# Joint x/gradient tile, an earlier reload of x, and stores issued by GpSimd and ScalarE, in a forward-and-backward block kernel

## The chip, the cores and the metric

The kernel runs on one core of a Trainium2 chip. The metric is device time in microseconds (us) from one launch to its end, median of several runs. A profiled execution gives a trace of every engine: TensorE (PE in the profile, its weight loads PEld), VectorE (DVE), ScalarE (ACT), GpSimd (POOL) and SyncE (SP). SP does no arithmetic here; it issues DMAs, one after the other in program order, and a DMA that must wait holds up all that stand behind it in SP's queue. The same holds for DMAs that ScalarE or GpSimd issue, in their own queues, with their arithmetic among them.

## The reference

The forward pass normalises x over its 512 features and adds three things: x itself, a gated long convolution over 2048 positions, and a gated bilinear feed-forward block. The kernel returns the output and the gradients of x, k, v, the two convolution kernels, the skip vector and the three weight matrices.

```python
def _A_ref(q, k, v, shift_k, ssm_k, ssm_D):
    k_shift = ...                      # 4-tap causal filter of k with shift_k
    kv = k_shift * v
    kv_f = rfft(pad(kv)); kf_f = rfft(pad(ssm_k))
    y = irfft(kv_f * kf_f)[:S]         # causal convolution over all 2048 positions
    y = y + kv * ssm_D
    return q * y

def _B_ref(x, w_gate, w_up, w_down):   # 512 -> 1376 -> 512
    h = (x @ w_gate) * (x @ w_up)
    return h @ w_down

xn = _layernorm(A_q)
out = A_q + _A_ref(xn, A_k, A_v, A_shift_k, A_ssm_k, A_ssm_D) + _B_ref(xn, B_w_gate, B_w_up, B_w_down)
# returned: out, and the vjp of out with grad_out for all inputs but B_x
```

All tensors are bf16; x, k, v and the gradient are 2048 x 512.

## The kernel before

The 2048 positions are laid out as 128 partitions with 16 rows each (`R`), and worked in 8 blocks of two rows (256 positions). Loads and stores of x, k, v, the gradient and the four results of that shape go through `load_rows` and `store_rows` (L212, L216): each is two DMAs of 64 partitions, issued by SP.

**Front.** For each block b, `load_q` and `load_go` (L299, L304) bring x and the gradient into tiles `x_b` and `go_b`; `norm_stats`, `norm_std` and `norm_rows` normalise x in place, and `store_xn` (L351) writes it to the DRAM scratch `XN`. `pre` (L380) multiplies gradient and normalised x (`dy_b`), filters k (`ks_b`, with the scratch tile `t_b`, stored to `KS`), and multiplies it by v (`v_b`). `stage1` (L364) runs the first stage of a two-stage Fourier transform by matmuls (`pf`), copies it to `fst` and stores it to the scratch `FD`. `kernel_spec` does the same for the convolution kernel, transposed by TensorE into tiles `kn`. `Tables` builds the sine tables on the chip: `W1` for the first stage, `EF` and `EI` for the second, `IW` for the inverse; `inverse_phases` does its part on GpSimd.

**Feed-forward.** For each block `ch`, `load_xt` (L486) brings normalised x and gradient transposed into `xt` and `gt` with transposing DMAs, from `x_b` and `go_b` while they are there, otherwise from `XN` and from the gradient's input tensor. The first two blocks are transposed by TensorE (`pe_t`, L469). `ffn1` multiplies by the three weights (`pgu`, `pdh`), forms the hidden values `hd` and stores them to the scratch `HDD`. `yb` (L543), which comes for block ch - 1 in the middle of `ffn1(ch)`, first reloads x into `xb` (one buffer), and then, for each of two halves, runs 11 matmuls of the down projection (`py`), adds x on VectorE (L554, into `bx`), and runs 22 matmuls of the gradient of the normalised x (`px`, L559). `bx` is stored to the scratch `BX`. `py` and `px` share two PSUM buffers.

**Second stage.** `groups` loads `X` from `FD`, transforms it (`ps`, `SP`), forms three products on VectorE (`T`, `U`, in `g_mul`), transforms back (`pg`, `GO`) and stores to the scratch `GD`. A generator interleaves this with the feed-forward work in TensorE's program order.

**Last phase.** When `ffn1` of the last block is done (tag `"wa"`), the gradient (`goC`) and `XN` (`xnC`) are loaded whole, 2 MB each (L884 to 887). Then `dw` (L1017) forms the three weight gradients, one block of 128 hidden features (`fb`) after another: `hb` holds all hidden values of that block, loaded from `HDD` (L787, two buffers), TensorE transposes them (`pt`, L843) and ScalarE copies them to `nath` and `natd`; `pd` and `pu` are the gradients, copied by ScalarE to `od` and `og` and stored by SP (L1007, L1046; `og` has one buffer and is stored after every second block). The last three blocks use transposing DMAs instead (`natT`, L797). Between these, `inv_y` and `inv_dk` load `GD` (`g1`, shown as `g`), transform it by matmuls (`pq`, `po`), and form `yC`, `dks` and the gradient of v (`kb`, in the buffer of the loaded `KS`, two buffers); `load_kh` loads k again (`khC`) for the gradient of the filter (`pk`); `final` (L1100) forms the output (`o`, one buffer) and the gradient of x (`e`, one buffer) with `bb`, loaded from `BX`; `bwd` (L1079) forms the gradient of k (`dk`, two buffers). `final` and `bwd` run wholly on VectorE, alternating, in `ew`; a rough order among generators is set by step counts (L1159), and a few DMAs are pinned behind another instruction (`issue_after`).

The program gives each DMA one of eight completion semaphores in turn. SP's and ScalarE's DMAs share one set of eight, and GpSimd's have their own. In the compiled order a DMA therefore also waits until the one eight before it in its set has landed.

## Time and profile before

| | us |
|---|---|
| median of 3 runs (lowest to highest) | 534.7 (534.37 to 536.45) |
| the profiled execution | 535.96 |
| its span, first to last instruction | 534.2 |
| TensorE busy | 480.1 (90%) |
| VectorE busy | 344.6 (65%) |
| ScalarE busy | 319.9 (60%) |
| GpSimd busy | 19.1 (4%) |

| moved by DMA | |
|---|---|
| all | 139.89 MB, mean 262 GB/s |
| queue of SP | 137.85 MB, 84.6% of the time of 16 DMA engines |
| queue of ScalarE | 1.36 MB, 1.0% |

The shares are averages over stages of quite different kinds. The front lasts till about 150 us, the interleaved second stage and feed-forward till about 345 us, and the last phase from there to the end. The profile cuts the span into 40 slices of 13.4 us and gives for each the busy share of every engine in tenths (9 is 90% or more), the clock granted to TensorE (PEclk), and the share of time in which the DMA engines were busy. A time line gives start, length, engine, line and operation, and in brackets the idle time of the engine ahead of it with what ended that idle time. SPq is SP's queue: its rows are the issues of DMAs, and a long one holds time in which the sequencer was held up.

### The profile page before, as it was taken

What the parts mean: (1) busy time and instruction counts of PE and PEld (TensorE: products, weight loads), DVE (VectorE), ACT (ScalarE), POOL (GpSimd) and SP (SyncE); (2) the same over time, 40 slices, a digit from 0 to 9 for tenths busy, and PEclk for the clock granted to TensorE, in tenths of its full rate; (3) what the DMA queues carried; (4) which work ended last, traced back from release to release, by engine and by line L of the source; (5) the groups of instructions that cost most, each with busy time, mean ns of one, the idle gap of its engine ahead of it and who ended that gap; (6) DMA issues with size and microseconds to landing.
All of it is one profiled execution on the core that took longest, in us unless ns stands there. A gap on an engine that the chain in (4) does not pass through costs nothing.

```text
span 534.2 us, 10803 instructions
## 1 busy us (share of the span) xinstructions
PE 480.1 (90%) x4438; PEld 316.4 (59%) x4438; DVE 344.6 (65%) x614; ACT 319.9 (60%) x354; POOL 19.1 (4%) x28
## 2 busy tenths in 40 slices
PE   6979999839993999999999999899987864999997
PEld 6957664414541664745736753366665644887776
DVE  5865777967828255777777776102246957797991
ACT  3757697734742677878969975176665512263332
POOL 9300000000000000000000000020000000000000
PEclk9989999987996999999999999899999997899999
DMA  9989966878799585997878469987999899969997
GB/s 249 337 250 260 312 213 213 294 216 294 255 337 254 191 239 192 269 259 250 231 254 291 151 173 306 371 302 219 356 330 331 272 214 312 333 147 261 259 243 235
DMA packets 106735, 139.89 MB, mean 262 GB/s; under 512 B 34715, under 2 KB 80192, under 8 KB 105150
## 3 DMA queue, kind: packets, MB, share of 16 engines
q1 hardware_dynamic: 105102, 137.85, 84.6%
q10 hardware_dynamic: 1584, 1.36, 1.0%
q8 instruction: 34, 0.56, 0.4%
q14 instruction: 15, 0.12, 0.1%
HBM read 68.45 MB, written 63.41 MB: 247 GB/s over the span
## 4 chain that ended last, share of the span: by engine, by line
PE 56%; DMA 15%; SPq 4%; ACT 2%; DVE 2%; issue 1%; DVEq 0%; ACTq 0%
PE pu L1035 12%; PE pgu L515 10%; PE px L559 10%; PE py L552 5%; PE pd L999 5%; DMA hb<-HDD 4%; PE pdh L521 4%; PE pt L843 3%; DMA g<-GD 3%; DMA khC<-in_A_k_dram 3%; DMA GD<-GO 2%; PE pg L617 2%; PE ps L588 2%; DMA xb<-in_A_q_dram 2%; SPq L497 2%; PE po L975 1%
## 5 line engine op out<-in xcount | busy, mean ns | idle before, releaser
L559 PE MATMUL px<-WT,hd 128*128 128x512 bf16 (+1 forms) x352 | 85.8, 394 | 15.3 <-DVE bx L554 14.7
L1035 PEld LDWEIGHTS <-xnC 128*128 128x128 bf16 x704 | 67.0, 98 | 9.0 <-issue 2.0
L559 PEld LDWEIGHTS <-hd 128*128 128x128 bf16 (+1 forms) x352 | 33.6, 101 | 61.3 <-issue 28.5
L1035 PE MATMUL pu<-natd,xnC 128*128 128x256 bf16 x512 | 58.3, 273 | 0.0
L234 ACT CAST GO<-pg 128x1024 bf16<-128x1024 f32 x48 | 46.2, 1015 | 15.4 <-issue 6.7
L604 DVE TENSOR_TENSOR T<-SP 128x2048 bf16<-128x2048 bf16 x24 | 29.4, 1223 | 38.8 <-ACT SP L234 38.8
L515 PE MATMUL pgu<-xt,Wu 128*128 128x256 bf16 (+1 forms) x352 | 53.9, 276 | 0.2 <-ACT gu L234 0.2
L234 ACT CAST gu<-pgu 128x1024 bf16<-128x1024 f32 (+1 forms) x48 | 45.3, 945 | 13.4 <-PE pgu L515 12.2
L515 PE MATMUL pgu<-xt,Wg 128*128 128x256 bf16 (+1 forms) x352 | 53.3, 274 | 0.0
L234 ACT CAST SP<-ps 128x1024 bf16<-128x1024 f32 x48 | 46.4, 1027 | 9.8 <-PE ps L588 7.9
L521 PE MATMUL pdh<-gt,WdT 128*128 128x256 bf16 (+1 forms) x352 | 47.1, 274 | 0.5 <-ACT gt L234 0.3
L552 PE MATMUL py<-Wd,hd 128*128 128x512 bf16 (+1 forms) x176 | 43.4, 390 | 3.9 <-DVE bx L554 2.3
L234 ACT CAST fst<-pf 128x1024 bf16<-128x1024 f32 x40 | 39.0, 1034 | 8.0 <-PE pf L372 5.5
L515 PEld LDWEIGHTS <-Wu 128*128 128x128 bf16 (+1 forms) x352 | 32.5, 101 | 16.7 <-issue 13.1
L234 ACT COPY natd<-pt 128x2048 bf16<-128x2048 bf16 x16 | 30.0, 1875 | 19.5 <-PE pt L843 19.5
L536 DVE TENSOR_TENSOR hd<-gu 128x512 bf16<-128x512 bf16 (+1 forms) x48 | 19.2, 399 | 32.0 <-ACT gu L234 32.0
L521 PEld LDWEIGHTS <-WdT 128*128 128x128 bf16 (+1 forms) x352 | 35.0, 101 | 6.0 <-issue 2.2
L515 PEld LDWEIGHTS <-Wg 128*128 128x128 bf16 (+1 forms) x352 | 35.1, 101 | 3.8
L552 PEld LDWEIGHTS <-hd 128*128 128x128 bf16 (+1 forms) x176 | 16.5, 99 | 27.2 <-issue 11.7
L843 PE MATMUL pt<-ident,hb 128*128 128x128 bf16 x336 | 23.9, 227 | 8.8 <-DMA hb<-HDD 8.8
L537 DVE TENSOR_TENSOR hd<-gu,dh 128x1024 bf16<-128x1024 bf16 (+1 forms) x48 | 30.9, 643 | 1.0
L234 ACT CAST og<-pu 128x1024 bf16<-128x1024 f32 (+1 forms) x11 | 10.9, 995 | 33.3 <-PE pu L1035 25.7
(167 smaller groups left out, 704.8 us busy)
## 6 DMA issues: line engine op xcount, KB each, us to landing
HDD<-hd SPq DMA_DIRECT2D x35, 384.0 KB, 4.4
FD<-fst SPq DMA_DIRECT2D x24, 512.0 KB, 3.9
X<-FD SPq DMA_DIRECT2D x24, 512.0 KB, 5.1
GD<-GO SPq DMA_DIRECT2D x24, 512.0 KB, 3.7
g<-GD SPq DMA_DIRECT2D x12, 1024.0 KB, 7.0
hb<-HDD SPq DMA_DIRECT2D x8, 1344.0 KB, 8.7
bb<-BX SPq DMA_DIRECT2D x8, 512.0 KB, 6.9
BX<-bx SPq DMA_DIRECT2D x7, 512.0 KB, 4.3
```

The costliest lines, as they stand in the source:

```text
L234: nc.scalar.copy(o, i)
L497: nc.sync.dma_start_transpose(out=t[:].rearrange("p r c s -> p (r c) s")[:, :, ss], in_=src.rearrange("p r d -> p (r d)"))
L515: nc.tensor.matmul(pgu[:w, i, t, :], lhsT=W[:, c, f0:f0 + w], rhs=xt[:, :, c, :], start=(c == 0), stop=(c == NC4 - 1))
L521: nc.tensor.matmul(pdh[:w, i, :], lhsT=WdT[:, c, f0:f0 + w], rhs=gt[:, :, c, :], start=(c == 0), stop=(c == NC4 - 1))
L536: nc.vector.tensor_tensor(hd[:fw, fb0:fb0 + n, 0, :], gu[:fw, :n, 0, :], gu[:fw, :n, 1, :], op=ALU.mult)
L537: nc.vector.tensor_tensor(hd[:fw, fb0:fb0 + n, 1:3, :], gu[:fw, :n], dh[:fw, :n].unsqueeze(2).to_broadcast((fw, n, 2, 256)), op=ALU.mult)
L552: nc.tensor.matmul(py[:], lhsT=hd[:fw, fb, 0, ss], rhs=Wd[:fw, fb, :], start=(fb == 0), stop=(fb == NFB - 1))
L559: nc.tensor.matmul(px[:], lhsT=hd[:fw, fb, t, ss], rhs=W[:fw, fb, :], start=(t == 1 and fb == 0), stop=(t == 2 and fb == NFB - 1))
L604: tt(W[:].rearrange("p c a d -> p c (a d)"), A[:, i:i + 1].rearrange("p c a d -> p c (a d)").to_broadcast((P, 2, 2 * D)), B[:].rearrange(" ...
L843: nc.tensor.transpose(pt[:, r, :fw], hs[:, (r % 2) * 128:(r % 2) * 128 + 128], ident[:fw, :fw])
L999: nc.tensor.matmul(pd[:fw, :], lhsT=nat_h(fb, r), rhs=goC[:, r, :], start=(r == 0), stop=(r == R - 1))
L1035: nc.tensor.matmul(pu[:, c, :, :fw], lhsT=xnC[:, r, cs(c)], rhs=nat_d(fb, r), start=(r == 0), stop=(r == R - 1))
```

## The change

- x and gradient of a block lie in one tile `xg` (four buffers, instead of four of x and three of the gradient), and `XN` holds both. `load_xt` issues one transposing DMA per block, and `pe_t` writes into the same joint tile. The closing load is `xgC` from `XN`, in two DMAs; the gradient is not read from its input again.
- `load_res` loads x for two feed-forward blocks at once (`xb` is twice as large, still one buffer). It is called at block 0, and from then on behind the second add of each odd block for the two that follow.
- `store_rows` issues from GpSimd: output, gradients of x, k and v. The stores of `od` and `og` issue from ScalarE.
- To make room, `dy_b` and `t_b` take the two buffers of `kn`, `W1` moves to the pool of the front, and a GpSimd table is computed in place.
- `load_halo` loads k in four DMAs instead of two. The first `bb` load is pinned behind the `kb` load of row 4 instead of a store.

```diff
-        W1 = self.tab.tile([P, 64, 2], BF, name="W1")
+        W1 = self.front.tile([P, 64, 2], BF, name="W1", bufs=1)
...
-        pb = tmp.tile([P, 16, 32], F32, name="pb")
-        e.tensor_scalar(pb[:], self.patR[:], self.gb[:, 0:1], None, op0=ALU.mult)
+        pb = self.patR
+        e.tensor_scalar(pb[:], pb[:], self.gb[:, 0:1], None, op0=ALU.mult)
...
     def store_rows(dst, rb, t):
         for h in range(2):
-            last = nc.sync.dma_start(dst[h, :, rb, :], t[hs(h)])
+            last = nc.gpsimd.dma_start(dst[h, :, rb, :], t[hs(h)])
...
-    XN = dram.tile([P, R, D], BF, name="XN")
+    XN = dram.tile([P, R, 2, D], BF, name="XN")
...
     def load_q(b):
-        x = stp.tile([P, 2, D], BF, name="x_b", bufs=4)
-        load_rows(x, x_n, slice(2 * b, 2 * b + 2))
-        return x
+        xg = stp.tile([P, 2, 2, D], BF, name="xg", bufs=4)
+        load_rows(xg[:, :, 0, :], x_n, slice(2 * b, 2 * b + 2))
+        return xg
 
-    def load_go(b, x):
-        go = stp.tile([P, 2, D], BF, name="go_b", bufs=3)
-        load_rows(go, go_n, slice(2 * b, 2 * b + 2))
-        XG[b] = (x, go)
+    def load_go(b, xg):
+        load_rows(xg[:, :, 1, :], go_n, slice(2 * b, 2 * b + 2))
+        XG[b] = (xg[:, :, 0, :], xg[:, :, 1, :], xg)
 
     def load_halo(t):
-        load_rows(t[:, 3:3 + R, :], k_n, slice(0, R))
+        for r0 in range(0, R, R // 2):
+            load_rows(t[:, 3 + r0:3 + r0 + R // 2, :], k_n, slice(r0, r0 + R // 2))
...
     def store_xn(b):
-        nc.sync.dma_start(XN[:, 2 * b:2 * b + 2, :], XG[b][0][:])
+        nc.sync.dma_start(XN[:, 2 * b:2 * b + 2], XG[b][2][:])
...
-        dy = ST["st1"].tile([P, 2, D], BF, name="dy_b")
+        dy = ST["st1"].tile([P, 2, D], BF, name="dy_b", tag="kn", bufs=KNB)
...
-        t = ST["st1"].tile([P, 2, D], BF, name="t_b")
+        t = ST["st1"].tile([P, 2, D], BF, name="t_b", tag="kn", bufs=KNB)
...
     def load_xt(ch):
...
-        xt = xtp.tile([P, 2, NC4, P], BF, name="xt")
-        gt = xtp.tile([P, 2, NC4, P], BF, name="gt")
...
-            nc.sync.dma_start_transpose(out=t[:].rearrange("p r c s -> p (r c) s")[:, :, ss], in_=src.rearrange("p r d -> p (r d)"))
+        XT[ch] = t = xtp.tile([P, 2, 2, NC4, P], BF, name="xgT")
+        src = XG[ch][2][:] if ch in XG else XN[:, 2 * ch:2 * ch + 2]
+        nc.sync.dma_start_transpose(out=t[:].rearrange("p r k c s -> p (r k c) s"), in_=src.rearrange("p r k d -> p (r k d)"))
...
+    def load_res(ch):
+        RES[0] = ybo.tile([P, 4, D], BF, name="xb", tag="xb", bufs=1)
+        load_rows(RES[0], x_n, slice(2 * ch, 2 * ch + 4))
+
     def yb(ch):
...
-        xb = ybo.tile([P, 2, D], BF, name="xb", tag="xb", bufs=1)
-        load_rows(xb, x_n, slice(2 * ch, 2 * ch + 2))
+        if ch == 0:
+            load_res(0)
+        xb = RES[0]
...
-                nc.vector.tensor_tensor(bx[:, sb, 0, :], py[:], xb[:, sb, :], op=ALU.add)
+                nc.vector.tensor_tensor(bx[:, sb, 0, :], py[:], xb[:, 2 * (ch % 2) + sb, :], op=ALU.add)
+            if sb == 1 and ch % 2 and ch < NCH - 1:
+                load_res(ch + 1)
...
-            xnC = c1.tile([P, R, D], BF, name="xnC")
-            goC = c1.tile([P, R, D], BF, name="goC")
-            load_rows(goC, go_n, slice(0, R))
-            nc.sync.dma_start(xnC[:], XN[:])
+            xgC = c1.tile([P, R, 2, D], BF, name="xgC")
+            for r0 in range(0, R, R // 2):
+                nc.sync.dma_start(xgC[:, r0:r0 + R // 2], XN[:, r0:r0 + R // 2])
+            xnC, goC = xgC[:, :, 0, :], xgC[:, :, 1, :]
...
-            nc.sync.dma_start(out_9[f0:f0 + fw, :], od[:fw])
+            nc.scalar.dma_start(out_9[f0:f0 + fw, :], od[:fw])
...
-                    nc.sync.dma_start(o[:, a:f0 + fw].rearrange("(c p) f -> p c f", p=128), og[:, t, :, :q0 + fw])
+                    nc.scalar.dma_start(o[:, a:f0 + fw].rearrange("(c p) f -> p c f", p=128), og[:, t, :, :q0 + fw])
...
-        with tc.issue_after(DKS[2].ins):
+        with tc.issue_after(DKS["kb", 4].ins):
             load_fin(0)
```

More of the change, by code (lines that the diff above doesn't have):

```diff
@@ L34, with __init__ @@
 class Tables:
-    def __init__(self, nc, tab, spectral, tmp):
+    def __init__(self, nc, tab, spectral, tmp, front):
         self.nc = nc
@@ L41, in __init__ @@
         self.tmp = tmp
+        self.front = front
         f = dict(allow_small_or_imprecise_dtypes=True)
@@ L103, in small_sin_w @@
     def small_sin_w(self):
-        self.W1 = self.tab.tile([P, 64, 2], BF, name="W1")
+        self.W1 = self.front.tile([P, 64, 2], BF, name="W1", bufs=1)
         self.sin(self.W1[:], self.tiw, 256)
@@ L467, with pe_t @@
     HD = {}
-    def pe_t(src, name, eng):
+    def pe_t(ch, k, eng):
+        src = XG[ch][k]
+        if ch not in XT:
+            XT[ch] = xtp.tile([P, 2, 2, NC4, P], BF, name="xgT")
         pt = P1("px8", [P, 2 * NC4, P], BF)
```

33 lines of the change are left out of this document (12 added, 21 removed).

## The prediction

> **What bounds the kernel now.** I read the slices of the span first, then who waited for whom, then the time lines of TensorE and of SP's queue.
>
> ```profile
> PE   6979999839993999999999999899987864999997
> PEclk9989999987996999999999999899999997899999
> DMA  9989966878799585997878469987999899969997
> ```
>
> TensorE (PE) works nearly without a break, save in slices 8 and 12 (107 to 120 us and 160 to 174 us) and in 31 to 33 (414 to 454 us). The DMA engines are about as full there as elsewhere. So I look at what TensorE waits for (columns: waiter, what it waited for, us in total, times, longest):
>
> ```profile
> PE px L559 <- DVE bx L554: 14.7, 2, 7.7
> DVE bx L554 <- DMA xb<-in_A_q_dram: 11.4, 3, 9.3
> PE pt L843 <- DMA hb<-HDD: 8.8, 2, 6.9
> PE pq L916 <- DMA g<-GD: 4.7, 2, 2.7
> PE pk L1058 <- DMA out_dram<-kb: 4.1, 1, 4.1
> ```
>
> The first two lines are one thing: the add of x to the down projection (L554) waits for the reload of x, `xb`, and holds a PSUM buffer that TensorE needs. A wait of 2.35 us at 341 us is its third case. The last three are the last phase: 8.8 + 4.7 + 4.1 = 17.6 us. TensorE's own rows show that the two long waits cost more than their length:
>
> ```profile
> 86.02 4.93 PE L559 MATMUL px<-WT,hd 128*128 128x512 bf16 x22
> ...
> 120.76 7.39 PE L559 MATMUL px<-WT,hd 128*128 128x512 bf16 x22 [6.97 <-DVE bx L554]
> ...
> 170.06 6.64 PE L559 MATMUL px<-WT,hd 128*128 128x512 bf16 x22 [7.70 <-DVE bx L554]
> ```
>
> The same 22 matmuls take 4.93 us without a wait ahead, 7.39 and 6.64 us behind the waits; the granted clock in these two stretches is 0.66 and 0.74. The two places hold 6.97 + 2.46 and 7.70 + 1.71, so 9.4 us each.
>
> Why the loads of the last phase are late is seen in SP's queue, which issues in order:
>
> ```profile
> 416.59 1.11 SPq L218 DMA_DIRECT2D out_dram<-e  x2
> 417.80 0.52 SPq L790 DMA_DIRECT2D hb<-HDD  x1
> ...
> 424.03 1.11 SPq L214 DMA_DIRECT2D khC<-in_A_k_dram  x2
> ...
> 429.57 10.62 SPq L218 DMA_DIRECT2D out_dram<-kb  x4
> ...
> 444.60 0.59 SPq L790 DMA_DIRECT2D hb<-HDD  x1
> ...
> SPq L218 <- DVE e L1124: 12.1, 3, 6.1
> ```
>
> Each `hb` load needs a buffer that ScalarE's last copy of an earlier block frees: the copies at 402.3 and 420.4 us. SP issues those loads at 417.8 and 444.6 us, 15 and 24 us later, right behind stores that wait for VectorE (`e`) or for a free DMA semaphore (`kb`, 10.62 us). TensorE then waits 1.93 us at 424 and 6.85 us at 453; the 4.1 us between them is `khC`, 14.5 us under way.
>
> **The change, part by part.** The sum is made on the profiled execution, 535.96 us with 534.2 us of span; the median of the runs is 534.7 us, 1.3 us lower.
>
> *Early reload of x.* One load serves two blocks and is issued behind the odd block's second add, 36 us before its use, not at the block's start behind transposes. The wait at 113.8 us goes. What is late next: TensorE would reach the `pf` matmuls of the convolution's front 9.4 us earlier, and there VectorE's `v_b` is ready only 1.6 us before TensorE takes it (126.5 against 128.1 us). VectorE itself idles 3.56 and 1.40 us for `KS` stores and 1.08 us for `xb` between 111 and 128 us, and only the last surely goes. So of 9.4 us I take 5 (bounds: 1.6 and 9.4). At 162.4 us nothing else is late: the products `T`, `U` that VectorE runs before the add come behind it in the compiled order; I take 8.5 of 9.4 (bounds: 0, if VectorE's 6.67 busy us in that gap stay ahead, and 9.4). At 341 us the first `hb` load, issued at 337.7 and needed at 346, is next: 1 of 2.35 us (bounds 0 and 2.35). Together 14.5 us. The reload's own wait for the add stands on SP ahead of a `v_b` load, `FD` and `XN` stores; before, the add is done (120 us) when SP comes to that place (126 us), so I cost it at nothing; without that cover it is one px pass, 4.9 us.
>
> *x and gradient in one tile.* For each of the 6 later blocks two or three transposing DMAs become one. In SP's time they were 13.0 us for `xt` and 18.6 us for `gt`; the 42-block one of the last phase takes 6.99 us, 0.17 us a block, so one of 16 blocks about 2.7 us, 6 of them 16 us: 15 us of SP's time less. TensorE stands only where counted above, so this adds nothing. `XN` doubles: 8 stores of 256 KB more, 2.1 MB at the mean 262 GB/s, 8.0 us of the DMA engines, and the `KS` store that VectorE waits for stands right behind each. Bounds 0 and 8; I take +3, as VectorE waited three times on `KS`. The closing load is 4 MB as before. The rows of x and gradient now land in pieces of 1 KB; the first wait for the gradient (2.82 us at 8.3 us) shows no such load, bounds 0 and another 2.8, taken as 0, since 128 KB loads of any kind here land in 3.4 to 4.1 us.
>
> *Smaller edits.* `dy_b` and `t_b` share the buffers of `kn`: the first block's chain moves from 56.7 us to behind the last use of `kn`, 68.2 us. TensorE takes its results at 77 and 81 us, so the `px` and `pw` matmuls between hide it; without them it is 8 us. `pb` in place, `W1` in another pool and halved `k` loads change no work; `k` comes some 2 us later behind an `XN` store, and VectorE first uses it at 56.7 us, 16 us after issue, against a landing of 12.
>
> *Stores of VectorE's results on GpSimd.* 64 issues leave SP: 16 x (0.54 + 0.57 + 0.59 + 0.54) = 36 us, with their waits for VectorE and the 10.6 us. The waits for `hb` (8.8) and `khC` (4.1) should go, those for `g` (4.7) hardly, since a `g` load still waits for the `hb` load eight DMAs ahead of it. But the DMA engines are full (the stretch; busy us of TensorE, its weight loads, VectorE, ScalarE, GpSimd; granted clock, DMA share, GB/s):
>
> ```profile
> 371.00:388.00 17.00, 15.73 (x146) 11.08 (x144) 2.69 (x4) 11.78 (x11) 0.00 (x0) 1.00 0.95 314
> 388.00:407.00 19.00, 15.61 (x146) 11.23 (x148) 9.04 (x20) 10.76 (x9) 0.00 (x0) 1.00 1.02 341
> ...
> 440.50:453.40 12.90, 6.01 (x81) 5.58 (x82) 9.65 (x24) 2.78 (x2) 0.00 (x0) 0.76 0.98 306
> 453.40:476.00 22.60, 22.60 (x260) 19.04 (x260) 19.45 (x41) 9.81 (x8) 0.00 (x0) 0.92 0.72 253
> 476.00:500.00 24.00, 24.00 (x217) 18.59 (x215) 20.41 (x45) 9.98 (x10) 0.00 (x0) 1.00 1.11 250
> 500.00:524.00 24.00, 24.00 (x249) 20.55 (x248) 22.38 (x41) 8.49 (x10) 0.00 (x0) 1.00 0.97 257
> ```
>
> The 24.4 MB from 371 to 453 us (with 274 and 241 GB/s in the two stretches left out) need 71 of their 82 us at 341 GB/s, the best stretch. So I take 9 us (bounds 0 and 17.6). GpSimd is idle here (19.1 us in all), but no row shows it issuing a DMA. By the nearest rows, SP's, 64 x 0.57 = 36 us are hidden by an idle engine; its own nearest, 19.1 us in 28 instructions, give 44 us; without cover VectorE would wait for its single buffers `o` and `e`, where it now waits 7.3 + 7.1 + 0.3 = 14.7 us. I take +2, bounds -14.7 and +30.
>
> *Stores of weight gradients on ScalarE.* 22 issues, 0.36 us by ScalarE's own row, 8 us, before copies `natd` that TensorE needs; ScalarE is busy 86 of 189 us. +1, bounds 0 and 8. Behind an `og` store that waits for its DMA semaphore stand those copies, too; the `hb` load that shares it lands before.
>
> Sum: 535.96 - 14.5 + 3 - 9 + 2 + 1 = 518.5 us, less 1.3 for the median: **517 us**.
>
> **Rivals.**
>
> *The transfers are the bound.* The stores compete with the loads wherever they are issued: the last phase gains nothing, 517 + 9 = 526, and if `XN` costs its whole 8 us as well, 531; I give 528. For it: the shares near 1. Against: buffers stood free for 15 and 24 us. The Trainium skill, "DMA: Bandwidth & Descriptors", section "Issuing engines are not separate DMA queues", says that issuing from another engine saves only the sequencer's time; this trace has DMA shares that fit it, and waits in SP's queue that are more than sequencer time.
>
> *The front's wait moves to VectorE.* TensorE, rid of `xb`, waits at `pf` and `ps` for VectorE and its `KS` buffers, and both gains there vanish but for 4 us: 517 + 9.5 = 526. For it: 1.6 us of slack. Against: VectorE is busy 31.0 of the 40 us from 80 to 120 us.
>
> *GpSimd's queue is the new bound (slower).* VectorE is busy 62.2 of the 70.6 us from 453.4 to 524 us (19.45 + 20.41 + 22.38 in the three stretches shown last above), and its last result is ready at 523.1 us, 8 us before TensorE's last matmuls end. If a pair of stores takes long enough that `o` and `e` come free late, VectorE waits in each of the 8 rounds of `final`. A round has about 8.5 us of other work behind `o`; a pair that lands later than that decides. At 4 us late in 8 rounds, 32 us: 517 + 32 - 8 = 541. For it: one buffer each. Against: SP's pairs land in 5.3 and 6.5 us. The Trainium skill, "SBUF — State Buffer", section "Who interferes with whom", has GpSimd's DMAs starved while VectorE runs in a two-port mode, and says `tensor_tensor` has none; VectorE's rows here, 0.69 us for 1024 elements of `tensor_tensor` and 0.54 us for 512 of L1123, cannot show it, as GpSimd issues no DMA before.
>
> *It does not do what it says.* SP stays late because `kb` loads wait for GpSimd's stores anyway: within 2.7 us of 534.7.
>
> **How the numbers follow.** Forecast 0.44, transfers 0.20, VectorE 0.15, GpSimd 0.15, no effect 0.06. 0.5% of 534.7 is 2.7 us, about what can be told from none. The forecast's own range is 505 to 525. All gains full, no costs: 534.7 - 38.8 = 496; to leave out 2 in 10, I cut that to 503, and take the upper end at 538, inside the slower rival. Faster: forecast, nearly all of the two cases at 526 and 528: 0.77; same 0.08; slower 0.15.
>
> **What would show it.** Right: no PE wait for `bx` at 113 and 162 us and 22 `px` matmuls in 4.9 us; `hb` issued within some 4 us of its freed buffer; PE idle in the last phase under 9 us. Wrong: `pf` waits of 5 us or more; VectorE's waits for `out_dram<-o`, `e` or `dk` above 15 us; long waits of ScalarE ahead of `natd`.

## The result

| | median, us | lowest to highest | executions |
|---|---|---|---|
| before | 536.17 | 532.91 to 540.18 | 20 |
| changed | 541.79 | 536.97 to 548.6 | 20 |

The ratio is 1.0097 with a 95% interval of 1.0074 to 1.012: the change makes the kernel 1% slower, where 517 us was forecast. The profiled execution of the changed kernel took 537.61 us with a span of 535.8 us, one of the shortest of its 20; a second profiled execution, below, took 539.03. The slices of the changed kernel's page, to be held against those of before:

```profile
PE   5989999894789799999999999999989944999994
PEclk8999999987889999999999999999999995999997
DMA  9999956879899786986879569999989996499955
```

Counted from 0, TensorE's gaps at slices 8 and 12 (107 to 120 and 160 to 174 us) have closed. That of the last phase now lies in slices 32 and 33 (428 to 455 us), both at 4 and the second with the clock at 0.5. A gap at slices 9 to 11 (121 to 161 us) is new. Where the time went is best seen in stages, cut at TensorE's first or last matmul of a kind; each number is a difference of start times that the trace gives for the groups `ps` (first), `pgu` (last), `px` (last) and `pd` (first and last), and 1.1 us lie between the third and the fourth.

| profiled execution, us | to the first `ps` | to the last `pgu` | to the last `px` | last phase | behind it | span |
|---|---|---|---|---|---|---|
| before | 157.0 | 154.7 | 39.7 | 177.8 | 3.9 | 534.2 |
| changed | 166.7 | 146.2 | 35.7 | 177.8 | 8.3 | 535.8 |
| changed, second profile | 164.7 | 146.2 | 35.7 | 183.2 | 6.4 | 537.3 |

The cut at the first `ps` does not part equal work: in the changed kernel TensorE does 212 matmuls of `py` and `px` ahead of it, before 202. Ten of them are about 2.2 us, by the 4.93 us that 22 take. With these on the same side, the second stage won some 6.3 us instead of 8.5, and the front lost some 7.5 us instead of 9.7. The third stage won 4.0 us, and the end lost another 4.4; the second profile loses 5.4 us in the last phase, too.

**The front.** TensorE's busy time (the second number after the stretch) before:

```profile
80.00:120.00 40.00, 30.16 (x171) 13.91 (x169) 30.95 (x60) 25.85 (x33) 0.00 (x0) 0.94 0.75 240
120.00:160.00 40.00, 36.97 (x250) 20.52 (x249) 24.23 (x48) 21.92 (x29) 0.00 (x0) 0.93 0.87 295
```

and of the changed kernel, with two stretches of the last phase:

```profile
80.00:120.00 40.00, 36.67 (x198) 16.79 (x196) 33.46 (x64) 24.04 (x32) 0.00 (x0) 0.96 0.72 245
120.00:160.00 40.00, 26.89 (x167) 16.02 (x166) 25.20 (x49) 19.94 (x26) 0.00 (x0) 0.83 0.89 291
425.00:454.00 29.00, 14.05 (x150) 10.85 (x150) 22.04 (x49) 6.30 (x5) 4.15 (x8) 0.79 0.87 320
500.00:536.00 36.00, 27.90 (x270) 22.95 (x268) 23.64 (x46) 8.06 (x10) 5.18 (x10) 0.92 0.61 183
```

TensorE wins 6.5 us up to 120 us and loses 10.1 us right after, at a granted clock of 0.83 instead of 0.93. What it waits for there, and for longest in the last phase, are these rows of its time line:

```profile
131.18 1.04 PE L372 MATMUL pf<-v_b,W 64*128 64x512 bf16 x4 [5.95 <-DVE v_b L403]
...
447.86 1.65 PE L846 MATMUL pt<-ident,hb 128*128 128x128 bf16 x14 [11.41 <-DVE kd L1066]
```

The wait for `bx` has turned into one for `v_b`, whose last block VectorE reaches at 152.3 us instead of 144.0.

**The last phase.** TensorE's waits from 345 us on (waiter, what it waited for, us in total, times, longest):

```profile
PE pt L846 <- DVE kd L1066: 12.7, 2, 11.4
PE pq L919 <- DMA g<-GD: 2.7, 1, 2.7
PE pk L1061 <- DMA khC<-in_A_k_dram: 2.3, 1, 2.3
```

That is 17.7 us, against 17.6 before. The wait for `hb` is gone, and TensorE now stands until VectorE has done `kd`, which frees a PSUM buffer. VectorE works in order and stands itself, for its stores (its waits from 345 us on):

```profile
DVE e L1115 <- DMA out_dram<-e: 18.7, 5, 5.5
...
DVE dk L1090 <- DMA out_dram<-dk: 7.6, 3, 3.5
DVE o L1111 <- DMA out_dram<-o: 6.3, 4, 3.2
```

These are 32.6 us, against 14.7 before, all of the growth at `e`. Of the 11.4 us that TensorE stands for `kd`, VectorE itself stands 2.5 us for `e` and 3.5 us for `dk`; in the rest it works at operations that its order has ahead of `kd`.

The stores of `e` did not become slower: from issue to landing, where the trace tells it, they took 2.2 to 8.5 us by SyncE before and 2.2 to 8.9 us by GpSimd in the changed kernel (medians 6.5 and 5.9). VectorE comes back to the buffer sooner. Here is its last operation on `e` of one block and the first of the next, before:

```profile
400.34 0.69 DVE L1124 TENSOR_TENSOR e<-e,goC 128x1024 bf16<-128x1024 bf16 x1
...
410.01 0.68 DVE L1112 TENSOR_TENSOR e<-goC,yC 128x1024 bf16<-128x1024 bf16 x1
```

and in the changed kernel:

```profile
396.39 0.68 DVE L1127 TENSOR_TENSOR e<-e,xgC 128x1024 bf16<-128x1024 bf16 x1
...
404.53 0.69 DVE L1115 TENSOR_TENSOR e<-xgC,yC 128x1024 bf16<-128x1024 bf16 x1 [5.54 <-DMA out_dram<-e]
```

Before, VectorE does six other operations between the two, 4.1 us of work, and some waits for other things; now two, 1.4 us, and then the wait for `e`. Over the seven rounds it is 6.7 us of other work on average before and 4.2 us in the changed kernel: VectorE's order is another.

### The profile page after: what moved, and what is told of

Read it like the earlier page. It is cut to its first block, busy times and chain, and to the rows that moved or that the text cites. A ratio compares the mean times of both kernels' runs of the same rounds, so it can differ in the third digit from the quotient of the medians.

```text
span 535.8 us, 10815 instructions
## 1 busy us (share of the span) xinstructions
PE 479.9 (90%) x4438; PEld 316.4 (59%) x4438; DVE 342.7 (64%) x614; ACT 320.4 (60%) x354; POOL 52.5 (10%) x92
## 3 DMA queue, kind: packets, MB, share of 16 engines
q1 hardware_dynamic: 93566, 127.42, 75.4%
## 4 chain that ended last, share of the span: by engine, by line
PE 50%; DMA 10%; DVE 7%; issue 3%; ACT 3%; POOL 1%; SPq 1%; ACTq 0%; DVEq 0%; POOLq 0%
PE pgu L509 10%; PE px L562 10%; PE pu L1038 8%; PE py L553 6%; PE pd L1002 4%; DMA out_dram<-o 3%; PE pdh L515 3%; PE pg L620 2%; PE ps L591 2%; PE pt L846 2%; DMA bb<-BX 2%; DMA out_dram<-og 1%; DMA kb<-KS 1%; DMA out_dram<-e 1%; PE po L978 1%
## 5 line engine op out<-in xcount | busy, mean ns | idle before, releaser
L1038 PEld LDWEIGHTS <-xgC 128*128 128x128 bf16 x704 | 67.0, 98 | 9.0 <-issue 2.0
L1038 PE MATMUL pu<-natd,xgC 128*128 128x256 bf16 x512 | 58.3, 273 | 0.0
L509 PE MATMUL pgu<-xgT,Wu 128*128 128x256 bf16 (+1 forms) x352 | 54.0, 277 | 4.0 <-ACT gu L235 3.1
L509 PE MATMUL pgu<-xgT,Wg 128*128 128x256 bf16 (+1 forms) x352 | 53.3, 274 | 0.0
L235 ACT CAST fst<-pf 128x1024 bf16<-128x1024 f32 x40 | 38.8, 1032 | 18.1 <-PE pf L372 17.7
L515 PE MATMUL pdh<-xgT,WdT 128*128 128x256 bf16 (+1 forms) x352 | 46.9, 276 | 2.3 <-ACT dh L235 1.8
L509 PEld LDWEIGHTS <-Wu 128*128 128x128 bf16 (+1 forms) x352 | 32.9, 101 | 20.4 <-issue 16.8
L955 POOL MEMSET dks<- 32x1536 bf16 x1 | 1.4, 1373 | 337.1 <-DMA BX<-bx 337.1
```

The lines of the kernel that those rows point to most:

```text
L235: nc.scalar.copy(o, i)
L509: nc.tensor.matmul(pgu[:w, i, t, :], lhsT=W[:, c, f0:f0 + w], rhs=xt[:, :, c, :], start=(c == 0), stop=(c == NC4 - 1))
L515: nc.tensor.matmul(pdh[:w, i, :], lhsT=WdT[:, c, f0:f0 + w], rhs=gt[:, :, c, :], start=(c == 0), stop=(c == NC4 - 1))
L1038: nc.tensor.matmul(pu[:, c, :, :fw], lhsT=xnC[:, r, cs(c)], rhs=nat_d(fb, r), start=(r == 0), stop=(r == R - 1))
```

## The experiments

Each ratio is to the kernel before, run beside it, with its 95% interval; it is not the quotient of two medians, and the median of the kernel before lay between 534.8 and 537.1 us in these sets. The changed kernel ran 20 times, the others 4 to 12 times. The order of work on an engine is planned anew for each kernel, and a store's queue is among what the plan depends on; where an order stayed the same, it is said.

| kernel | median, us | ratio | interval |
|---|---|---|---|
| changed kernel | 541.79 | 1.0097 | 1.0074 to 1.012 |
| changed, all stores by SyncE | 534.46 | 0.9956 | 0.9931 to 0.9981 |
| before, with the store moves alone | 547.4 | 1.0138 | 1.0094 to 1.0182 |
| changed, only ScalarE's stores moved | 541.14 | 1.0066 | 1.0027 to 1.0105 |
| changed, only GpSimd's stores moved | 542.22 | 1.0107 | 1.0058 to 1.0156 |
| before, with shared buffers | 537.99 | 1.0025 | 1.0 to 1.005 |
| ... and the early reload | 532.01 | 0.9941 | 0.9908 to 0.9974 |
| ... and the joint tile instead of the reload | 534.48 | 0.9978 | 0.9952 to 1.0005 |
| changed, two buffers for `e` | 541.42 | 1.0092 | 1.0061 to 1.0122 |
| changed, `kd` ahead | 540.6 | 1.0074 | 1.005 to 1.0098 |
| all stores by SyncE, `KS` by GpSimd | 530.36 | 0.9877 | 0.986 to 0.9895 |
| early reload without the joint tile, `KS` by GpSimd | 529.68 | 0.9865 | 0.9847 to 0.9882 |
| all by SyncE, weight gradients by GpSimd | 538.09 | 1.005 | 1.0024 to 1.0077 |
| only GpSimd's stores moved, the last ones by SyncE | 541.42 | 1.0131 | 1.0089 to 1.0172 |
| changed, `bb` loads by GpSimd | 549.85 | 1.0263 | 1.0214 to 1.0312 |
| the 529.68 us kernel, `bb` loads by GpSimd | 533.16 | 0.9919 | 0.9887 to 0.9951 |
| changed, `KS` by GpSimd | 539.04 | 1.0038 | 1.0007 to 1.0069 |
| the 529.68 us kernel, `kb` stores by GpSimd | 522.79 | 0.9764 | 0.9727 to 0.9802 |

### Taking the change apart

All stores back to SyncE:

```diff
-            last = nc.gpsimd.dma_start(dst[h, :, rb, :], t[hs(h)])
+            last = nc.sync.dma_start(dst[h, :, rb, :], t[hs(h)])
...
-            nc.scalar.dma_start(out_9[f0:f0 + fw, :], od[:fw])
+            nc.sync.dma_start(out_9[f0:f0 + fw, :], od[:fw])
...
-                    nc.scalar.dma_start(o[:, a:f0 + fw].rearrange("(c p) f -> p c f", p=128), og[:, t, :, :q0 + fw])
+                    nc.sync.dma_start(o[:, a:f0 + fw].rearrange("(c p) f -> p c f", p=128), og[:, t, :, :q0 + fw])
```

> The changed kernel with every store of the last phase issued by SyncE again; the joint tile, the buffers that dy and t share with kn, and the early reload stay. Theory (the store moves cost, in the tail and in VectorE's waits): TensorE reaches the last phase 2.8 us earlier than before the change (last px 348.6 against 351.4 us), and VectorE's tail behind TensorE's last matmul goes back from 8.3 to about 4 us, so about 533 us, 0.5% below the kernel before and some 1.5% below the changed one; VectorE's waits for stores fall from 32.6 to about 15 us, and waits for hb come back in the last phase. Rival 1 (the front's rearrangement is what costs): the time stays at the changed kernel's 542 us. Rival 2 (the doubled XN, now read back whole as xgC, clogs the transfers at the head of the last phase): 540 us or more, with the loss between 345 and 425 us.

Measured: 0.9956. The theory holds: 534.46 - 541.79 = -7.3 us come back with the stores. TensorE's order is that of the changed kernel; VectorE's is the same for the first 409 of its 614 operations and another behind them, so that this run undoes the queues and the order together. VectorE's waits for its stores here:

```profile
DVE o L1111 <- DMA out_dram<-o: 7.5, 3, 3.6
DVE dk L1090 <- DMA out_dram<-dk: 7.1, 3, 5.8
```

There is none for `e`, and the time behind TensorE's last matmul is 4.0 us. The other way round, the kernel before with these three lines and the gate of the first `bb` load as changed:

> The kernel before with the store moves alone: VectorE's results by GpSimd, weight gradients by ScalarE, the first bb load gated by the kb load of rows 4. Theory (the store moves cost): slower than before by about what the tail and VectorE's store waits add, 4 to 8 us, so 540 to 544 us; VectorE's waits for stores of o, e and dk above 25 us, its last dk 5 us later. Rival 1 (the front's parts cost): 536 us as before. Rival 2 (freeing SyncE of the stores was right, as the prediction had it, and the front takes it away): 525 to 530 us.

Measured: 1.0138, more than the theory's price; TensorE waits 16.1 us for `kd` at 453 us, and VectorE 36 us for its stores. Then each half of the move by itself. Only ScalarE's stores moved (the first line of the diff undone alone):

> The changed kernel with only the stores of VectorE's results (o, e, dk, kb) issued by SyncE again; od and og stay with ScalarE. Theory (GpSimd's stores land late and hold VectorE's single buffers, about two thirds of the loss): 535 to 537 us, VectorE's waits for stores near 15 us, and the 8.9 us wait of ScalarE behind og's issue stays. Rival (ScalarE's blocked issue is what costs, by way of dks and VectorE): 540 us or more, VectorE's waits for ScalarE's dd as in the changed kernel.

Only GpSimd's stores moved (the other two lines undone):

> The changed kernel with od and og stored by SyncE again and VectorE's results still by GpSimd. Theory, now that putting GpSimd's stores back alone left 541 us and putting both back gave 534.5 us (ScalarE's issues cost most, since ScalarE stands at og's issue until a load of SyncE's has landed): 532 to 536 us, no ScalarE wait for khC, no TensorE wait of 11 us for kd; GpSimd's stores then cost 0 to 2 us. Rival (the two moves cost alike and not in sum): 538 to 541 us, with VectorE's waits for stores near 30 us as in the changed kernel.

Measured: 1.0066 and 1.0107. Against 0.9956, the halves alone cost 1.1% and 1.5%, and both together 1.4%. Both theories that gave one half the blame fell; the second rival, alike and not in sum, comes nearest. With GpSimd's half alone TensorE waits 16.8 us for `kd`; with ScalarE's half alone that wait is not there, but `e` waits 10.8 us, and the end comes 7.3 us behind the last matmul. Here, too, VectorE's order is not that of the kernel with all stores by SyncE; the first 455 operations are the same.

The front, by parts. The buffers of `dy` and `t` alone, on the kernel before:

```diff
-        dy = ST["st1"].tile([P, 2, D], BF, name="dy_b")
+        dy = ST["st1"].tile([P, 2, D], BF, name="dy_b", tag="kn", bufs=KNB)
...
-        t = ST["st1"].tile([P, 2, D], BF, name="t_b")
+        t = ST["st1"].tile([P, 2, D], BF, name="t_b", tag="kn", bufs=KNB)
```

> The kernel before with dy and t of the front in kn's two buffers, as in the changed kernel, and nothing else. Theory (the sharing delays the front's VectorE chain: t of a block waits for the TensorE matmul that reads dy): the last v_b some 7 to 10 us later than 144.0 us, TensorE waits of 5 us or more for v_b with a lower granted clock behind them, and the front's end (last pgu 311.7 us) later by 5 us or more, so 541 to 546 us. Rival (the doubled XN ahead of KS delays it): last v_b within 2 us of 144.0 us, 536 us.

Measured: 1.0025. The first `v_b` comes 11.3 us later (75.4 against 64.1 us), the last only 1.9 us. The theory fell. With these buffers, the early reload (`load_res` and its calls as in the change, with the small edits for its room and the halved loads of `k`):

> The kernel before with the early reload of x and the buffers that dy and t share with kn (needed for its room), but with x and gradient in separate tiles, XN of half the size, and all stores by SyncE. Theory (the early reload is right, and what cancels it in the front is the joint tile with the doubled XN): the waits of TensorE for bx at 120.8, 170 and 341 us go, the last v_b stays near 146 us as in the run with the shared buffers alone, and some 6 to 10 us are gained: 526 to 531 us. Rival 1 (the front is bound by VectorE's chain, whatever is reloaded early, and the bx waits only move to v_b): the last v_b at 146 us, but a TensorE wait of 5 us for v_b in place of the bx wait at 120 us; the waits at 170 and 341 us still go, 530 to 534 us. Rival 2 (the early reload itself delays VectorE's chain, by its 512 KB beside KS and X): last v_b after 150 us, 535 us or more.

and instead the joint tile (all stores back, and the reload as before):

> The changed kernel without the early reload and with all stores by SyncE: the joint tile with the doubled XN and the shared buffers alone. Theory (the doubled XN delays KS and with it VectorE's chain): last v_b at 151 us or later against 146 us with the shared buffers alone, VectorE's waits for KS 9 us or more against 5.6 us, bx waits of TensorE at 120 and 170 us as before; 541 to 546 us. Rival (the joint tile costs nothing; it is the early reload that delays the chain): last v_b near 146 us, 536 to 539 us.

Measured: 0.9941 and 0.9978. The reload is worth 0.8% (0.9941 against 1.0025, intervals apart). Its 532.0 us and a wait of 4.6 us for `v_b` at 126 us are rival 1's: the wait for `bx` moves. The joint tile costs nothing by itself; its theory fell, the time lies even below the rival's, and its last `v_b` came at 146.0 us. But both together are not better than the reload alone (0.9956 against 0.9941), with the last `v_b` at 154.2 us.

### What holds VectorE in the front

SyncE's queue in the changed kernel, and below it VectorE's row:

```profile
116.07 0.35 SPq L352 DMA_DIRECT2D XN<-xg  x1
116.46 0.57 SPq L378 DMA_DIRECT2D FD<-fst  x1
117.08 0.68 SPq L401 DMA_DIRECT2D KS<-ks_b  x1
...
129.17 0.35 SPq L352 DMA_DIRECT2D XN<-xg  x1
129.58 0.42 SPq L401 DMA_DIRECT2D KS<-ks_b  x1
```

```profile
121.95 0.69 DVE L393 TENSOR_TENSOR ks_b<-kh,skb 128x1024 bf16<-128x1024 bf16 x1 [3.98 <-DMA KS<-ks_b]
```

SyncE stood 3.6 us before this `XN` store, for VectorE's normalising of a later block. The `KS` store is issued behind it. VectorE had written the last of what it stores by 103.1 us, 14.0 us before this issue, and VectorE's next `ks_b` waits until it has landed, 4.9 us after its issue. That is a ring: VectorE, `XN`, `KS`, VectorE. To break it, one line, on the changed kernel with all stores by SyncE and on the early reload without the joint tile:

```diff
-        nc.sync.dma_start(KS[:, 2 * b:2 * b + 2, :], ks[:])
+        nc.gpsimd.dma_start(KS[:, 2 * b:2 * b + 2, :], ks[:])
```

> The changed kernel with the last phase's stores by SyncE, and the front's KS store moved from SyncE to GpSimd. In the runs so far the joint tile alone left the last v_b at 146 us, the early reload alone at 147 us, both together at 154 us. Theory A (a ring: VectorE's ks waits for a KS store that stands in SyncE's queue behind XN's store, which waits for VectorE's normalising): VectorE's waits for KS fall from 10.5 to under 4 us, the last v_b comes at 148 us or before, TensorE's 5.3 us wait for v_b at 132 us goes, and the time falls from 534.5 to 528 to 531 us. Rival B (TensorE and ScalarE pace VectorE's chain there; the KS wait only takes up slack): the last v_b stays after 151 us, and the time within 2 us of 534.5. Rival C (GpSimd's store is slower to land than SyncE's and the wait grows): 536 us or more.

> The kernel before with the early reload and the shared buffers (532 us) and the front's KS store by GpSimd; tiles of x and gradient separate, stores of the last phase by SyncE. Theory A (the ring through SyncE): VectorE's waits for KS fall from 6.4 to under 3 us, the 4.6 us wait of TensorE for v_b goes, 527 to 530 us, which would beat both kernels. Rival B (slack only): 531 to 533 us.

Measured: 0.9877 and 0.9865, 0.8% better than the same kernels without it, intervals apart; both beat the kernel before. VectorE's wait for `KS` from 75 to 158 us in the changed kernel with all stores by SyncE:

```profile
DVE ks_b L393 <- DMA KS<-ks_b: 10.5, 5, 3.7
```

and with `KS` by GpSimd:

```profile
DVE ks_b L393 <- DMA KS<-ks_b: 2.6, 1, 2.6
```

The store of the same block now goes out 3.2 us after it is ready. In these two profiles the last `pgu`, up to which TensorE's work is the same, starts at 308.3 instead of 316.4 us. (The first `ps` starts at 161.5 instead of 168.6 us, but a group of 11 `py` matmuls has moved behind it.) TensorE's longest wait for `v_b` falls from 5.3 to 4.1 us, all of them together do not: 8.9 and 9.6 us. The line also changes VectorE's order, from its 103rd operation on. So that this line gains is shown, and that it takes VectorE's waits for `KS` away; how much of the gain is the ring's and how much the new order's is not. By the medians it is 4.1 us, less than half of what the front falls short by (below). The same line on the changed kernel as it stands:

> The changed kernel with the front's KS store by GpSimd and nothing else. Theory A (front and last phase add up: the ring through SyncE is worth 4 to 6 us, and the last phase's loss stays): 535 to 538 us, ratio to the kernel before 0.999 to 1.004. Rival B (the last phase takes the gain up, since the transfers of the last phase's head bound it): 540 us or more.

Measured: 1.0038 against 1.0097. By the ratios front and last phase add up, though the time is a little above the theory's 535 to 538 us. Its profile does not show the place: the last `pgu` starts at 312.3 us, against 312.9 and 310.9 us in the two profiles of the changed kernel.

### What the stores cost in the last phase

Two buffers for `e` (its pool `c2b` instead of `c2`); TensorE's order stays, VectorE's nearly:

> The changed kernel with two buffers for e in place of one; TensorE's order is the same, VectorE's nearly. Theory A (GpSimd's stores land late and VectorE, in order, stands at e and holds kd, pk's PSUM buffer and the end behind it): VectorE's waits for out_dram<-e fall from 18.7 us to under 5 us, TensorE's wait for kd from 11.4 to under 7 us, and 4 to 6 us come back: 535 to 538 us. Rival B (the waits for e only stand where others would: bb, dk and o come next): the waits for dk, o and bb grow by as much, 540 to 543 us as the changed kernel.

Measured: 1.0092, no gain. VectorE's waits from 350 us on:

```profile
DVE o L1111 <- DMA out_dram<-o: 20.0, 5, 8.7
...
DVE e L1115 <- DMA out_dram<-e: 12.2, 3, 6.8
```

The wait moved from `e` to `o`, as rival B has it: the buffer by itself is not the price. Taking `kd` ahead (its multiplication at high priority in the plan):

> The changed kernel with kd taken ahead of VectorE's other work in the planned order; TensorE's order is the same, VectorE's last phase is planned anew. Theory A (TensorE's wait for kd is half of the loss): that wait falls from 11.4 to under 4 us, but VectorE's waits for the stores stay near 30 us and with them the 8 us behind TensorE's last matmul: 537 to 540 us. Rival B (TensorE's waits in the last phase are taken up by the next wait, for hb or g, and VectorE's end sets the end): 541 to 543 us.

Measured: 1.0074; the wait for `kd` stayed at 11.0 us, so `kd` did not come earlier, and the run does not decide.

Is it ScalarE's blocked issue? In the changed kernel ScalarE stands 8.9 us before `og` (422 to 431 us):

```profile
ACT og L235 <- DMA khC<-in_A_k_dram: 8.9, 1, 8.9
```

The name in this row misleads. A part of that load was the last to land on a semaphore that it shares with the stores of `og`. But ScalarE goes on at 430.89 us, 0.1 us after the `og` store that it had issued at 414.54 us has landed: `og` has one buffer, and this store took 16.3 us. In the second profile the same wait (7.4 us) ends 0.1 us behind the landing of the same store, and is put down to it:

```profile
ACT og L235 <- DMA out_dram<-og: 15.2, 3, 7.4
```

So where the expectations here and above let ScalarE stand for a load of SyncE's, they follow a wrong name; ScalarE stood for its own store. With `od` and `og` by GpSimd instead, everything else by SyncE; the orders of TensorE, VectorE and SyncE are those of the kernel with ScalarE's half alone:

> The changed kernel with VectorE's results stored by SyncE and the weight gradients (od, og) by GpSimd in place of ScalarE. TensorE's, VectorE's and SyncE's orders are those of the run with ScalarE's stores alone (541.1 us, 1.0066 of the kernel before); the queue of these stores is the only difference. Theory A (ScalarE's issue is the cost: it stands, in order, until a completion semaphore that it shares with SyncE's loads is free, and holds the drains behind it): the time falls to that with all stores by SyncE, 533 to 536 us (0.9956 of the kernel before), TensorE's wait for pk at 442 us is 4 us or less. Rival B (what costs is that these stores leave SyncE's queue, so that the loads behind them start earlier and VectorE's order changes): 539 to 542 us, as with ScalarE. Rival C (GpSimd's stores of 256 KB are slow to land and og has one buffer): 543 us or more, waits of ScalarE for out_dram<-og over 10 us.

Measured: 1.005, where ScalarE gave 1.0066 and SyncE 0.9956. The first two are not told apart. This is nearer to rival B: these stores cost about as much from GpSimd. Nor is ScalarE's stand at `og` the price: with ScalarE's half alone there is none at this place, only waits of 2.9 and 6.0 us later on (2.8 and 6.1 us by GpSimd), against one of 5.5 us with all stores by SyncE. What both kernels share, and the one with all stores by SyncE does not, is VectorE's order. The last stores back to SyncE:

```diff
-            last = nc.gpsimd.dma_start(dst[h, :, rb, :], t[hs(h)])
+            last = (nc.sync if rb.start >= 12 and dst is not o3_n else nc.gpsimd).dma_start(dst[h, :, rb, :], t[hs(h)])
```

> The changed kernel with od and og by SyncE, VectorE's results by GpSimd except the o, e and dk stores of the last two blocks, by SyncE again. Theory A (the end of the program waits 2 to 3 us for GpSimd's last store after every other engine is done): 2 to 4 us less than the same kernel with those stores by GpSimd (542.2 us), so 538 to 540 us, and no wait for out_dram<-dk at the end. Rival B (the end waits as long for whatever store is last): 541 to 543 us.

Measured: 1.0131, no gain. The program of the changed kernel waits at its end for the last `dk` store:

```profile
SPq L1196 <- DMA out_dram<-dk: 2.0, 1, 2.0
```

With the store moved, this wait is gone, and the end comes 5.2 us behind TensorE's last matmul, against 9.0 us with GpSimd's half alone, but the time does not fall. The profile of this run is its slowest (546.91 us), so it does not show where the time goes instead.

The changed kernel once more:

> The changed kernel once more, one look: its profiled execution above was among the fastest of its 20. Theory (a typical execution loses 4 to 5 us more at one place of the last phase, where TensorE waits for a load that stands in SyncE's queue behind a bb load waiting for VectorE): 540 to 544 us with TensorE waits for natT or dDt between 480 and 520 us. Rival (the difference is spread, by the clock): the same waits as before and a granted clock lower by 0.01.

539.03 us, with two rows of TensorE that the first profile doesn't have:

```profile
496.41 3.18 PE L1002 MATMUL pd<-xgC,natT 128*128 128x512 bf16 x13 [0.95 <-DVE dDt L238]
510.14 2.97 PE L1002 MATMUL pd<-xgC,natT 128*128 128x512 bf16 x13 [1.01 <-DMA natT<-HDD]
```

They are the theory's waits, but with 2 us of waits they explain only part of the 5.4 us that the last phase is longer; the wait for `g` grew from 2.7 to 5.7 us as well. Then the `bb` loads by GpSimd as well, on the changed kernel and on the fastest one:

```diff
-        nc.sync.dma_start(bb[:], BX[:, 2 * b:2 * b + 2, :, :])
+        nc.gpsimd.dma_start(bb[:], BX[:, 2 * b:2 * b + 2, :, :])
```

> The changed kernel with the bb loads issued by GpSimd too. Theory S (freed of the stores, SyncE runs ahead to the bb loads, stands there 20 us and 16 us in the repeated look until VectorE has freed a buffer, and holds g, hb and natT behind it): those waits of SyncE go, TensorE's waits for g (5.7 us) and natT and dDt (2 us) fall under 2 us in sum, and the time comes to 534 to 538 us. Rival B (what costs is VectorE's planned order and its waits for the stores; SyncE's standing is slack): 539 to 543 us, TensorE's wait for kd still near 11 us.

> The fastest kernel so far (early reload, separate tiles, KS by GpSimd, last phase's stores by SyncE; 529.7 us, 0.9865 of the kernel before) with the bb loads by GpSimd. Theory S (loads that wait for VectorE belong on a queue of their own, behind which nothing else stands): 525 to 529 us, TensorE's waits for hb and g in the last phase, 15 us now, under 10 us. Rival B (as with every other move off SyncE's queue in the last phase, VectorE's order changes for the worse): 533 to 537 us.

Measured: 1.0263 and 0.9919 (from 1.0097 and 0.9865): worse both times. Theory S fell: to free SyncE of its standing at `bb` wins nothing. Last, only the 16 `kb` stores by GpSimd:

```diff
-            last = nc.sync.dma_start(dst[h, :, rb, :], t[hs(h)])
+            last = (nc.gpsimd if dst is o3_n else nc.sync).dma_start(dst[h, :, rb, :], t[hs(h)])
```

> The fastest kernel so far (0.9865 of the kernel before) with the 16 kb stores alone issued by GpSimd; those of o, e, dk, od and og stay with SyncE. It takes from SyncE's queue the 10.6 us stand on which the prediction built its gain for the last phase. Theory (kb has two buffers and its stores come early, so their landing holds nobody; what costs is moving o and e, which have one buffer each): 526 to 530 us, TensorE's waits for pk and hb, 9 us now, under 5 us. Rival (any of these moves lets SyncE run ahead and changes VectorE's order for the worse): 532 us or more.

Measured: 0.9764, the fastest kernel of the study, 522.79 us; the time is even below the theory's. TensorE's waits from 345 us on without this line:

```profile
PE pt L854 <- DMA hb<-HDD: 5.6, 1, 5.6
PE pq L927 <- DMA g<-GD: 5.0, 2, 4.1
PE pk L1069 <- DMA out_dram<-kb: 3.5, 1, 3.5
```

and with it:

```profile
PE pk L1069 <- DMA bb<-BX: 4.4, 1, 4.4
PE pt L854 <- DMA hb<-HDD: 2.0, 1, 2.0
PE pq L927 <- DMA g<-GD: 1.0, 1, 1.0
PE pq L927 <- ACT od L235: 0.7, 1, 0.7
PE po L986 <- DMA g<-GD: 0.3, 1, 0.3
```

14.1 us have become 8.4, and VectorE has no wait at `e`; those for `pk` and `hb` are 6.4 us, not under 5 as expected. (`pk` reads `khC`, whose last load lands within 0.4 us of this wait's end in both; the rows name a DMA that landed beside it.) In the profiled executions the last phase shrinks from 178.1 to 168.0 us, but they exaggerate: the one with the line is the shortest of its 7 (518.13 us), the one without it the longest of its 4 (530.18 us). TensorE's order is the same in both; VectorE's is the same for the first 433 operations only, so that here, too, queue and order changed together.

## Why the prediction was wrong

**The step that failed first is the last phase: "I take 9 us (bounds 0 and 17.6)" for SyncE freed of the stores, with +2 and +1 for GpSimd's and ScalarE's issuing.** In sum it gave -6 us. Measured, all stores moved against none is 1.0097 / 0.9956 = 1.0142, some +7.6 us. The step treated 64 + 22 stores as one thing, a row of issues in front of loads, and gave the 9 us no bound on the side of a loss. The runs showed two things in it. The `kb` stores, at which SyncE stood 10.6 us, were worth moving: 0.9764 / 0.9865 = 0.9898, or -5.4 us, and on the loads named, `hb`, `g` and `khC`. The stores of `o`, `e` and `dk` were not: with them moved too, VectorE's waits for its stores more than double, `kd` comes late, and TensorE's 17.6 us of waits change their name only. The prediction took VectorE's order of work as given; it changed, and VectorE came back to `e` after 4.2 us of other work instead of 6.7. That these three are the costly ones follows from the difference between two sets of runs on different fronts; none of them was moved alone.

**The early reload (-14.5 us) was right in two of three places.** At 162 us 8.5 us were taken and some 6.3 came; that the table has 8.5, too, is chance, since 2.2 us of it are matmuls that moved ahead of the cut. At 341 us 4.0 us came where 1 was taken, but the joint tile without the reload has the same 35.7 us there, so the reload can't claim them alone. At 113 us, -5 became some +7.5. The prediction had the number that decides, 1.6 us of slack at `v_b`, and VectorE's waits for `KS`, and still took a gain as its lower bound. It missed that TensorE's wait had been the time in which VectorE, paced by the `KS` ring, caught up: without it TensorE comes early and waits for `v_b`. This is read from the traces; with `KS` by GpSimd these waits stay (9.6 us), so the ring is not all of it. This is the rival "the front's wait moves to VectorE", in its place and its cause; its price, 9.5 us, was short, since the chain itself became 8.3 us later. The whole front, with all stores by SyncE, is worth 0.4% (2.4 us) instead of 11.5, so it falls short by 9.1 us.

**The doubled `XN` (+3)** showed no cost of its own: 0.9978 with the joint tile, 1.0025 without. Only beside the reload is it in doubt (0.9956 against 0.9941, not told apart). **The shared buffers (0)** were right: the first block moved as worked out, and 0.25% is at the edge of what the interval can tell from nothing.

**GpSimd's path (+2, bounds -14.7 and +30)** was mis-sized: alone it costs 1.0107 / 0.9956, +8.1 us. The slower rival named the place, VectorE waiting for the single buffers, but not the reason: it has the stores of `e` land late, and they landed as soon as SyncE's. Its reckoning, 4 us late in 8 rounds, isn't what happened either: the waits grew by 17.9 us, not 32, and they took effect through `kd` and TensorE. That its 541 us is the time that came is luck, since it keeps 13.5 us of gains in the front and at 162 us, most of which didn't come. **ScalarE's stores (+1, bounds 0 and 8)** were mis-sized, too: alone +1.1%, 5.9 us. It looked for the wait at a semaphore shared with a load; ScalarE's wait in the changed kernel was for the one buffer of `og`, whose store took 16.3 us to land. With ScalarE's half alone that wait is not there, and the same stores by GpSimd cost 0.9% (1.005 / 0.9956), so the stand itself is little of it.

Of the signs that were to show it wrong, two came: a `pf` wait of 5.95 us, and 32.6 us of VectorE's waits for its stores. Of those that were to show it right, TensorE's waits for `bx` are gone; its idle time in the last phase, 17.7 us, is not under 9.

Two readings in the prediction were off. Not 128 KB loads "of any kind" landed in 3.4 to 4.1 us: those of `vb` took 6.0. The first wait for the gradient, at which nothing was put for this reason, is 4.2 us instead of 2.8 (3.4 in the second profile, but as much with the shared buffers alone). And TensorE's transposes free a buffer of `hb`, not ScalarE's copies, which begin when these end; the times are the same.

The Trainium skill, "DMA: Bandwidth & Descriptors", section "Issuing engines are not separate DMA queues", expects from another issuing engine only the sequencer's time. The times here moved in both directions, +1.4% for all stores and -1.0% for `kb` alone, but VectorE's order moved with them, so that these runs do not test it. In the one pair with the same orders on TensorE, VectorE and SyncE, `od` and `og` by ScalarE or by GpSimd, 1.0066 and 1.005 are not told apart, which fits it.

**What stays open.** Why `od` and `og` cost 1% whichever engine but SyncE issues them is not shown. When a store leaves SyncE's queue, the loads behind it go out earlier and VectorE's order is planned anew; no run takes a store off SyncE and holds VectorE's order fixed. The profiled executions also lie low for some of these kernels (532.35 us of a median of 538.09 for the weight gradients by GpSimd), so a single profile places the loss only in part.

## What to carry to other kernels

Before moving a DMA to another queue, ask for each store on its own what waits behind it in the queue and what waits for its landing: `kb`, with two buffers and a queue standing behind it, gained 1.0%, and all stores together lost 1.4%. Where a planner orders the work, compare the order of each engine before and after: here the waits at `e` grew though its stores landed no later. When a wait is put down to a DMA, look whether the engine goes on when that DMA lands. A wait that TensorE loses is worth its length only if the engine that comes next has slack; look for rings through an in-order queue first (VectorE, `XN`, `KS`, VectorE), since one line that breaks the ring gave 0.6 to 0.8%. Move one kind at a time and measure each: parts that are good alone (0.9941 and 0.9978) were no better together (0.9956).

## What the runs showed of the hardware that was not expected

- In ten profiled executions of nine kernels whose order of work differs only behind the front, the first `ps` comes at 163.9 to 171.5 us; stages of a few us can't be told apart from one profile.
- Queues of two engines that use completion semaphores in turn hold each other up. In the second profile a `khC` load of SyncE's waits for ScalarE's `og` store, which has the same semaphore, and is issued when that lands, at 431.97 us:

```profile
SPq L314 <- DMA out_dram<-og: 9.4, 1, 9.4
```

- An `og` store of 256 KB landed 9.9 us after its issue by ScalarE (median; 13.9 us in the second profile, 5.5 us with ScalarE's half alone), 3.9 us by SyncE, with the same bytes. GpSimd needed 0.52 us to issue a 128 KB store, and its stores landed in 3.6 to 6.8 us (medians of the four kinds), with all stores by SyncE in 2.4 to 6.0. VectorE's operations beside them kept their length: 0.69 us for 1024 elements of `tensor_tensor`.
